# Half-filled contraction chunks in a conditioned attention and feed-forward block: zero padding to 128 rows, a new order of half and full matmuls, and a rebuilt passage between the two parts

## Chip, cores, metric

One core of one Trainium2 chip. The metric is the device time of one execution in microseconds (us). Times are quoted as the median and the range of the runs. A ratio is the mean time of one kernel's runs over that of the other's in the same rounds, so it is not quite the ratio of the medians that I quote. The span of a profiled execution is some 1.7 us shorter than the time of the same run (488.3 against 490.01 for the kernel before); spans are compared with spans and times with times.

Words used below: PE is TensorE's matmul, PEld its weight load, DVE VectorE, ACT ScalarE, POOL GpSimd. The "passage" is the time from the last key/value tile of attention to the first matmul of the feed-forward part (FFN). The "fold" multiplies the key and query weights by w_phi at the start, with "block weights" that GpSimd makes; a "num group" is the ten matmuls that give one tile's attention numerators; an "eviction" copies a matmul's result out of PSUM; a "half pair" is two matmuls of 64 rows side by side.

## The reference

```python
S, D, H, Dh, Dff = 2048, 576, 32, 18, 4608          # bf16 inputs, one batch
mod = silu(c) @ w_mod                                # six vectors sa, ca, ga, sb, cb, gb of 576
h = layernorm(x) * (1 + ca) + sa
q, k, v = split(h @ wqkv)                            # 32 heads of 18
phi(u) = concat(softmax(u @ w_phi), softmax(-u @ w_phi))
kv, z = phi(k)^T v, sum_s phi(k)                     # linear attention
o = (phi(q) kv) / (phi(q) z + 1e-6)
x = x + ga * (o @ wo)
h = layernorm(x) * (1 + cb) + sb
x = x + gb * (relu(h @ w1) @ w2)
```

What matters is that D = 576 = 4 x 128 + 64. Both kernels contract over at most 128 rows in one matmul, so each product over D has four full chunks and a half one of 64 rows.

## The kernel before

The half chunk is packed. Two 64-row matmuls, one on rows 0 to 63 and one on rows 64 to 127, go to two outputs and run side by side. The weights' last 64 rows therefore lie in SBUF twice.

```python
def paired(ps, lhs, rhs, splits, first=True):        # k, v, output projection
    for bk, (c0, cn) in enumerate(splits):
        for ci in range(4):
            nc.tensor.matmul(ps(bk)[:, 0:cn], lhsT=lhs(ci, 0, P), rhs=rhs[:, ci, c0:c0 + cn], ...)
    for bk, (c0, cn) in enumerate(splits):
        b0 = 64 * bk
        nc.tensor.matmul(ps(bk)[:, 0:cn], lhsT=lhs(4, b0, b0 + 64), rhs=rhs[b0:b0 + 64, 4, c0:c0 + cn], ...)

def mod_columns(parts, dst, psum):                   # one-column matmuls: 2 parts x 6 column groups x 5 chunks
    ...
                    for ck in range(NC):
                        k = KR[ck]                   # 128, 128, 128, 128, 64
                        nc.tensor.matmul(ps[p0:p0 + pn, n * NC + ci:n * NC + ci + 1],
                                         lhsT=wmod_sb[i][0:k, ck, ci * P:ci * P + pn], rhs=siluc[0:k, ck:ck + 1], ...)

def ffn(b, steps):                                   # b = 0..4; blocks of 256, 512, 512, 512, 256 tokens
    ...
    for j in range(NJ // 2):                         # 18 steps
        pace(9 * nn / 2400)                          # other tiles' work is inserted here by an estimate of time
        pair = (j, j + NJ // 2)
        for n, jj in enumerate(pair):                # eight full matmuls
            for ci in range(4):
                nc.tensor.matmul(hps[n][:, 0:nn], lhsT=w1a[:, ci, jj * P:(jj + 1) * P], rhs=h2T[:, ci, 0:nn], ...)
        for n in range(2):                           # then one half pair
            b0 = 64 * n
            nc.tensor.matmul(hps[n][:, 0:nn], lhsT=w1b[b0:b0 + 64, j * P:(j + 1) * P],
                             rhs=h2T[b0:b0 + 64, 4, 0:nn], start=False, stop=True)
        for n, jj in enumerate(pair):                # Relu: one on ScalarE, one on VectorE
            ...
```

While the FFN runs on block b, the attention output of block b+1 (`num_tile`, `tr_tile`, `wo_tile`) is inserted into TensorE's stream. Tiles 0 and 1 have no FFN to hide behind: they make up the passage.

The softmax here doesn't subtract the row's maximum and nothing guards it: scores larger than these inputs give would overflow.

Of the kernel before, what the change touches and what calls it, by code (L numbers as in the profile page):

```python
# [8 lines left out]
P = 128  # L9
# [9 lines left out]
NC = 5  # L19
# [16 lines left out]
def kernel(  # L36
# [74 lines left out]
    xn = small([P, NX, D], BF16, "xn")  # L111
# [7 lines left out]
    o_sb = small([P, NO, D], BF16, "o_sb")  # L119
# [11 lines left out]
    def load_rows(eng, dst, src, dup):  # L131
        eng.dma_start(dst[:, 0:4, :], src[0:512, :].rearrange("(k p) n -> p k n", p=P))
        eng.dma_start(dst[0:64, 4, :], src[512:576, :])
        if dup:
            eng.dma_start(dst[64:128, 4, :], src[512:576, :])
# [4 lines left out]
    for k in range(NC):  # L140
# [3 lines left out]
    load_rows(nc.sync, wmod_sb[0], w_mod[:, 0:D], False)  # L144
    load_rows(nc.sync, wmod_sb[1], w_mod[:, D:2 * D], False)
    load_rows(nc.sync, wv_sb, A_wqkv[:, 2 * D:3 * D], True)
    nc.sync.dma_start(x_sb[:, 4:8, :], xf[:, 4:8, :])
    load_rows(nc.sync, wq_raw, A_wqkv[:, 0:D], False)
    nc.sync.dma_start(x_sb[:, 8:16, :], xf[:, 8:16, :])
    load_rows(nc.sync, wmod_sb[2], w_mod[:, 2 * D:3 * D], False)  # L150
    load_rows(nc.sync, wo_sb, A_wo, True)
# [9 lines left out]
                            base=DH - 1, pattern=[[DH, 7]], channel_multiplier=-1)  # L161
    nc.gpsimd.memset(v_sb[:, :, 0:4, 126:127], 1.0)
# [25 lines left out]
    KR = [128, 128, 128, 128, 64]  # L188

    def mod_columns(parts, dst, psum):  # L190
        ps = psum()
        for n, i in enumerate(parts):
            for ci in range(NC):
                for p0, pn in ((0, P),) if ci < 4 else ((0, 64), (64, 64)):
                    for ck in range(NC):
                        k = KR[ck]
                        nc.tensor.matmul(ps[p0:p0 + pn, n * NC + ci:n * NC + ci + 1],  # L197
                                         lhsT=wmod_sb[i][0:k, ck, ci * P:ci * P + pn], rhs=siluc[0:k, ck:ck + 1],
                                         start=(ck == 0), stop=(ck == NC - 1))
        nc.vector.tensor_copy(out=dst[:, 0, :], in_=ps[:, 0:NC])  # L200
        nc.vector.tensor_scalar(out=dst[:, 1, :], in0=ps[:, NC:2 * NC], scalar1=1.0, scalar2=None, op0=ALU.add)

    def mod_row(i, dst, psum):
        for hf in range(2):
            ps = psum()
            for ck in range(NC):
                k = KR[ck]
                nc.tensor.matmul(ps[:, 0:HD2], lhsT=rep[0:k, ck, :],
                                 rhs=wmod_sb[i][0:k, ck, hf * HD2:(hf + 1) * HD2],
                                 start=(ck == 0), stop=(ck == NC - 1))  # L210
            nc.scalar.activation(out=dst[:, hf * HD2:(hf + 1) * HD2], in_=ps[:, 0:HD2], func=ACT.Copy)
# [9 lines left out]
    def fold_transposes(raw, dstT, engs):  # L221
        t0, t1 = two(), two()
        pts = [p.bitcast(BF16) for p in (t0[:, 0, :], t0[:, 1, :], t1[:, 0, :], t1[:, 1, :], one())]
        for ci in range(NC):
            for g, (h0, nh) in enumerate(GRP):
                f0, nf = h0 * DH, nh * DH
                if ci < 4:
                    nc.tensor.transpose(pts[g][0:nf, ci * P:(ci + 1) * P], raw[:, ci, f0:f0 + nf], ident[:, :])
                else:
                    for r in range(2):  # L230
                        nc.tensor.transpose(pts[g][0:nf, 512 + 64 * r:576 + 64 * r], raw[0:64, 4, f0:f0 + nf],
                                            ident[0:64, 0:64])
        for g, (h0, nh) in enumerate(GRP):
            nf = nh * DH
            if engs[g % len(engs)] == "a":
                nc.scalar.activation(out=dstT[0:nf, g, :], in_=pts[g][0:nf, 0:640], func=ACT.Copy)
            else:
                nc.vector.tensor_copy(out=dstT[0:nf, g, :], in_=pts[g][0:nf, 0:640])
# [27 lines left out]
    def ln_apply(n, t):  # L266
        return nc.vector.tensor_scalar(out=xn[:, t % NX, :], in0=x_sb[:, t, :],
                                scalar1=rs[:, n, t, 0:1], scalar2=rs[:, n, t, 1:2],
                                op0=ALU.mult, op1=ALU.add)
# [3 lines left out]
    def feat_t(t0, nt, psum, n):  # L273
        pt = psum().bitcast(BF16).rearrange("p (c f) -> p c f", c=2)
        for k, ci in enumerate(CS[n]):
            for j in range(nt):
                x = xn[:, (t0 + j) % NX, :]
                if ci < 4:
                    nc.tensor.transpose(pt[:, k, j * P:(j + 1) * P], x[:, ci * P:(ci + 1) * P], ident[:, :])  # L279
                else:  # L280
                    for r in range(2):
                        nc.tensor.transpose(pt[64 * r:64 * r + 64, k, j * P:(j + 1) * P], x[:, 512:576], ident[:, :])  # L282
# [16 lines left out]
    def paired(ps, lhs, rhs, splits, first=True):  # L299
        for bk, (c0, cn) in enumerate(splits):  # L300
            for ci in range(4):
                nc.tensor.matmul(ps(bk)[:, 0:cn], lhsT=lhs(ci, 0, P), rhs=rhs[:, ci, c0:c0 + cn],  # L302
                                 start=(first and ci == 0), stop=False)
        for bk, (c0, cn) in enumerate(splits):
            b0 = 64 * bk
            nc.tensor.matmul(ps(bk)[:, 0:cn], lhsT=lhs(4, b0, b0 + 64), rhs=rhs[b0:b0 + 64, 4, c0:c0 + cn],  # L306
                             start=False, stop=True)
# [4 lines left out]
    def k_tile(t):  # L312
        ps = two()
        paired(lambda bk: ps[:, bk, :], lambda ci, a, b: hT[a:b, ci, t * P:(t + 1) * P], wk_sb, HALF)
# [5 lines left out]
    def v_tile(t):  # L320
        ps = two()
        paired(lambda bk: ps[:, bk, :], lambda ci, a, b: hT[a:b, ci, t * P:(t + 1) * P], wv_sb, VSPL)
# [5 lines left out]
    def k_softmax(t):  # L328
# [8 lines left out]
        for sgn, eng in ((1, nc.gpsimd), (0, nc.vector)):  # L337
# [5 lines left out]
    def kv_tile(t):  # L343
        for g, (h0, nh) in enumerate(GRP):
            f0, nf = h0 * DH, nh * DH
            for sgn in range(2):
# [20 lines left out]
    def q_mm(b, n, psum):  # L367
        sl = slice(b * TB, (b + 1) * TB)
        pss = psum(len(QG[n]))
        for k, g in enumerate(QG[n]):  # L370
            f0, nf = GRP[g][0] * DH, GRP[g][1] * DH
            for ci in range(4):
                nc.tensor.matmul(pss[k][0:nf, :], lhsT=wq_sb[:, ci, f0:f0 + nf], rhs=hT[:, ci, sl],  # L373
                                 start=(ci == 0), stop=False)
        for k, g in enumerate(QG[n]):
            f0, nf = GRP[g][0] * DH, GRP[g][1] * DH
            b0 = 64 * k
            nc.tensor.matmul(pss[k][0:nf, :], lhsT=wq_sb[b0:b0 + 64, 4, f0:f0 + nf],  # L378
                             rhs=hT[b0:b0 + 64, 4, sl], start=False, stop=True)
# [39 lines left out]
    for n in range(3):  # L419
        feat_e(pts[n], 4, hT, 0, mod1, "vavav", n)  # L420
    order.close()
    nc.sync.dma_start(wmod_sb[3][:, 0:4, :], w_mod[0:512, 3 * D:4 * D].rearrange("(k p) n -> p k n", p=P))
    nc.sync.dma_start(wmod_sb[3][0:64, 4, :], w_mod[512:576, 3 * D:4 * D])
    load_rows(nc.sync, wmod_sb[5], w_mod[:, 5 * D:6 * D], False)

    QT = {4: (0, 0), 5: (0, 1), 7: (0, 2), 8: (1, 0), 9: (1, 1), 11: (1, 2), 12: (2, 0), 13: (2, 1), 15: (2, 2)}

    def a_filler(t):
        if t == 0:
            fold_transposes(wq_raw, wqT, "av")  # L430
            load_rows(nc.sync, wmod_sb[4], w_mod[:, 4 * D:5 * D], False)
# [12 lines left out]
    for t in range(NT + 1):  # L444
        if t < NT:
# [3 lines left out]
            if u < NT:  # L449
# [6 lines left out]
                if u % 4 == 3:  # L456
                    to_features(u - 3, 4, one, hT, (u - 3) * P, mod1, "avava", 0)
# [4 lines left out]
        if t < NT:  # L462
            if t + 4 < NT and t % 4 == 3:
                for n in (1, 2):
                    to_features(t + 1, 4, one, hT, (t + 1) * P, mod1, "avava", n)
# [4 lines left out]
    kv_tile(NT - 1)  # L470
    for k in range(2):
        q_exp(3, 0, q3[0], k)
    for g in range(NG):
        kv_final(g)
    actx.close()
# [13 lines left out]
    bctx = ExitStack()  # L489
    n3 = bctx.enter_context(tc.tile_pool(name="n3", bufs=2, space=PS, reuse_waits="tile"))  # L490
    s1 = bctx.enter_context(tc.tile_pool(name="s1", bufs=2, space=PS, reuse_waits="tile"))
# [16 lines left out]
    def num_mm(t, psum):  # L508
# [7 lines left out]
        for sgn in range(2):  # L516
            for g in range(3):
# [18 lines left out]
    def num_o(t, ps, adder):  # L536
# [22 lines left out]
        adder.tensor_tensor(out=o_sb[:, t % NO, :], in0=tm[:, 0, :], in1=tm[:, 1, :], op=ALU.add)  # L559
# [6 lines left out]
    def tr_tile(t, psum):  # L566
        pt = psum().bitcast(BF16)
        ot = o_sb[:, t % NO, :]
        for ci in range(4):
            nc.tensor.transpose(pt[:, ci * P:(ci + 1) * P], ot[:, ci * P:(ci + 1) * P], ident[:, :])  # L570
        for r in range(2):
            nc.tensor.transpose(pt[64 * r:64 * r + 64, 512:640], ot[:, 512:576], ident[:, :])  # L572
        nc.scalar.activation(out=oT[:, t % NO].rearrange("p c f -> p (c f)"), in_=pt[:, 0:640], func=ACT.Copy)  # L573

    def wo_mm(t, pss, first=True):
        f = oT[:, t % NO]
        paired(lambda bk: pss[bk], lambda ci, a, b: f[a:b, ci, :], wo_sb, HALF, first=first)
# [29 lines left out]
    def feat(b, n, psum):  # L607
        t0, nt = FB[b]
        to_features(t0, nt, psum, h2T, 0, mod2, "vavav", n)

    def ffn(b, steps):
# [11 lines left out]
        for j in range(NJ // 2):  # L623
            pace(9 * nn / 2400)
            pair = (j, j + NJ // 2)
            hps = [psf(), psf()]
            for n, jj in enumerate(pair):
                for ci in range(4):
                    nc.tensor.matmul(hps[n][:, 0:nn], lhsT=w1a[:, ci, jj * P:(jj + 1) * P], rhs=h2T[:, ci, 0:nn],  # L629
                                     start=(ci == 0), stop=False)  # L630
            for n in range(2):
                b0 = 64 * n
                nc.tensor.matmul(hps[n][:, 0:nn], lhsT=w1b[b0:b0 + 64, j * P:(j + 1) * P],  # L633
                                 rhs=h2T[b0:b0 + 64, 4, 0:nn], start=False, stop=True)
            for n, jj in enumerate(pair):
                if n == 0:
# [32 lines left out]
    def q_n3(n):  # L669
        ps = num3()  # L670
        return [ps[:, i, :] for i in range(n)]

    nps = [num_mm(0, num3)]
    num_d(0, nps[0])
    q3[1] = q_mm(3, 1, q_n3)
    num_o(0, nps[0], nc.vector)
    q_exp(3, 1, q3[1], 0)
    tr_tile(0, one_a)
    nps.append(num_mm(1, num3))
    num_d(1, nps[1])  # L680
    q_exp(3, 1, q3[1], 1)
    xps = [wo_x_mm(0, num3)]
    wo_mm(0, [xps[0][:, i, :] for i in range(2)], first=False)
    num_o(1, nps[1], nc.vector)
# [3 lines left out]
    mod_columns((3, 4), mod2, one_a)  # L688
    tr_tile(1, one_a)
    xps.append(wo_x_mm(1, num3))  # L690
    wo_mm(1, [xps[1][:, i, :] for i in range(2)], first=False)
    wo_x_stats(1, xps[1])
    ln_rstd(1, 1, 2)
    ln_apply(1, 1)
    mod_row(5, gb_row, one_a)
    q3[2] = q_mm(3, 2, lambda n: [one_a()])
# [65 lines left out]
```

## Time and profile before

| | kernel before |
|---|---|
| time, median of 15 runs | 488.58 us (487.25 to 490.8) |
| span of the profiled run, mean granted clock | 488.3 us, 0.965 |
| last key/value tile ends | 114.2 us |
| first FFN matmul | 140.2 us |
| first matmul of FFN block 1 (the first with 512 columns) | 195.8 us |

The profile's main lines are in the prediction. To read a row of stages: the stretch in us from the start, its length, then busy us of PE, PEld, DVE, ACT and POOL with the number of instructions, then the granted clock of TensorE (1.00 is full, 0.50 half), then DMA share and GB/s. These are the rows of the kernel before. The marks are the start of VectorE's key softmax (its sum, L331) for tile 0 and for tile 4, the end of the last key/value tile, the first FFN matmul, and the first of FFN block 1:

```profile
24.50:53.20 28.70, 23.34 (x205) 14.90 (x205) 24.93 (x57) 16.51 (x47) 5.12 (x4) 0.88 0.25 75
53.20:114.20 61.00, 59.67 (x476) 36.60 (x475) 38.21 (x48) 42.31 (x88) 18.42 (x12) 1.00 0.24 89
...
140.20:196.00 55.80, 53.17 (x443) 37.17 (x443) 30.10 (x87) 14.76 (x45) 5.61 (x4) 0.94 0.22 76
196.00:488.30 292.30, 288.06 (x2036) 175.31 (x2046) 124.25 (x289) 59.48 (x138) 14.05 (x10) 1.00 0.03 9
```

The first row, the passage (in the prediction) and the third have a clock below 1; the long row has PE busy for 288 of 292 us at full clock.

### The profile page before, as it was taken

The page shows a single profiled execution, that of the slowest core. Times are in us where ns is not written, and L with a number is a line of the kernel's source. Part 1 is how long each engine was busy: PE and PEld are TensorE (multiplying, and loading weights), DVE is VectorE, ACT ScalarE, POOL GpSimd, SP SyncE. Part 2 cuts the span into 40 slices and gives each one's busy share as a digit, 9 for nine tenths or more (in the row PEclk, how much of TensorE's full clock was granted, in tenths as well). Part 3 has the DMA queues.
Part 4 walks back from the last instruction along what each step waited for, and adds up shares of the span by engine and source line. Part 5 has one row for each costly group of instructions (what it writes and reads, how often), then busy time and mean ns, then how long its engine had stood idle before and what let it go on. Part 6 is the DMA issues. An engine that isn't in the chain of part 4 may idle for free.

```text
span 488.3 us, 8270 instructions
## 1 busy us (share of the span) xinstructions
PE 464.0 (95%) x3506; PEld 292.3 (60%) x3518; DVE 243.5 (50%) x565; ACT 154.2 (32%) x367; POOL 48.1 (10%) x59
## 2 busy tenths in 40 slices
PE   7978999997869999999999999999999999999997
PEld 6654566564536677334677733467773337777675
DVE  4597865656545654323655433365543332654312
ACT  4465686574333321223211122221112220112300
POOL 3012132231001110000211000021100000110000
PEclk9598999998888999999999999999999999999999
DMA  8950550000084000000000000000000000000000
GB/s 234 343 178 1 219 217 1 1 1 3 1 304 132 1 0 14 13 0 1 0 13 13 13 13 1 0 1 13 13 13 12 1 0 1 26 12 13 1 1 25
DMA packets 17312, 22.67 MB, mean 46 GB/s; under 512 B 2043, under 2 KB 16635, under 8 KB 16763
## 3 DMA queue, kind: packets, MB, share of 16 engines
q1 hardware_dynamic: 16064, 22.12, 13.6%
q8 instruction: 27, 0.44, 0.4%
q10 hardware_dynamic: 1210, 0.02, 0.2%
q14 instruction: 11, 0.08, 0.1%
HBM read 19.78 MB, written 2.36 MB: 45 GB/s over the span
## 4 chain that ended last, share of the span: by engine, by line
PE 72%; ACT 1%; DVE 1%; POOL 0%; issue 0%; POOLq 0%
PE psf L647 30%; PE psf L629 28%; PE psf L633 5%; PE psf L302 3%; PE num L514 2%; PE s L197 1%; PE pt L570 1%; PE psf L306 1%; PE psf L279 1%; PE n L302 1%; PE pt L572 1%; POOL o_sb L559 0%; PE psf L282 0%; DVE h2T L293 0%; ACT h2T L290 0%
## 5 line engine op out<-in xcount | busy, mean ns | idle before, releaser
L629 PE MATMUL psf<-h2T,rW 128*128 128x512 bf16 (+1 forms) x708 | 142.3, 341 | 1.1 <-DVE h2T L293 0.5
L647 PEld LDWEIGHTS <-rH 128*128 128x128 bf16 x1152 | 109.2, 98 | 29.6 <-issue 0.7
L647 PE MATMUL psf<-rW,rH 128*128 128x288 bf16 x864 | 116.8, 286 | 0.0
L639 DVE TENSOR_SCALAR rH<-psf 128x512 bf16<-128x512 f32 (+1 forms) x90 | 52.4, 583 | 97.4 <-PE psf L633 97.4
L629 PEld LDWEIGHTS <-rW 128*128 128x128 bf16 x720 | 64.4, 99 | 58.0 <-issue 11.9
L637 ACT ACTIVATE rH<-psf 128x512 bf16<-128x512 f32 (+1 forms) x90 | 46.1, 512 | 127.3 <-PE psf L633 127.3
L559 POOL TENSOR_TENSOR o_sb<-rV 128x576 bf16<-128x576 f32 x14 | 19.7, 1405 | 296.1 <-DVE rV L555 296.1
L302 PE MATMUL two<-rW,rH 128*128 128x288 bf16 (+2 forms) x256 | 42.8, 309 | 2.3 <-DVE rH L252 0.7
L650 DVE TENSOR_TENSOR yt<-psf,gb_row 128x288 f32<-128x288 f32 x32 | 14.5, 454 | 60.4 <-PE psf L647 60.4
L647 PE MATMUL psf<-rEQ,rH 128*128 128x288 bf16 x288 | 41.0, 286 | 0.0
L331 DVE TENSOR_REDUCE R_sb<-rH 128x64 f32<-128x1152 bf16 x16 | 21.6, 1351 | 23.8 <-ACT rH L317 23.7
L302 PEld LDWEIGHTS <-rH 128*128 128x128 bf16 x256 | 24.1, 104 | 14.0 <-issue 3.9
L339 POOL TENSOR_TENSOR rH<-rH,R_sb 128x576 bf16<-128x576 bf16 x16 | 23.5, 1474 | 81.2 <-ACT R_sb L334 41.5
L633 PE MATMUL psf<-h2T,rW 64*128 64x512 bf16 (+1 forms) x180 | 31.4, 346 | 0.0
L633 PEld LDWEIGHTS <-rW 64*128 64x128 bf16 x180 | 8.6, 93 | 30.9 <-issue 30.9
L261 ACT ACTIVATE rs<-mv,eps_t 128x1 f32<-128x1 f32 (+2 forms) x24 | 7.1, 294 | 62.7 <-DVE mv L258 60.2
L257 DVE BATCH_NORM_STATS2 st<-x_sb 128x6 f32<-128x288 bf16 x60 | 24.3, 439 | 3.3 <-DMA x_sb<-in_A_x_dram 3.3
L317 ACT ACTIVATE rH<-two 128x576 bf16<-128x576 f32 x32 | 19.3, 663 | 9.0 <-PE two L306 7.8
L386 ACT ACTIVATE rEQ<-two 126x512 bf16<-126x512 f32 (+1 forms) x34 | 17.7, 600 | 11.6 <-PE two L378 11.6
L573 ACT ACTIVATE oT<-pt 128x640 bf16<-128x640 bf16 x14 | 9.9, 704 | 35.6 <-PE pt L572 35.3
L339 DVE TENSOR_TENSOR rH<-rH,R_sb 128x576 bf16<-128x576 bf16 x16 | 17.5, 1096 | 0.7
L373 PE MATMUL two<-rH 128*126 128x512 bf16 (+1 forms) x68 | 16.5, 382 | 0.6 <-ACT rH L317 0.6
(135 smaller groups left out, 407.5 us busy)
## 6 DMA issues: line engine op xcount, KB each, us to landing
rW<-in_B_w_dram SPq DMA_DIRECT2D x1, 4608.0 KB
rW<-in_B_w_dram SPq DMA_DIRECT2D x3, 1296.0 KB, 9.0
rW<-in_w_mod_dram SPq DMA_DIRECT2D x6, 576.0 KB, 8.0
out_dram<-x_sb SPq DMA_DIRECT2D x16, 144.0 KB, 1.7
rEQ<-in_B_w_dram SPq DMA_DIRECT2D x1, 1296.0 KB
rW<-in_A_wqkv_dram SPq DMA_DIRECT2D x2, 576.0 KB, 9.7
x_sb<-in_A_x_dram SPq DMA_DIRECT2D x1, 1152.0 KB, 10.2
rW<-in_A_wqkv_dram SPq DMA_DIRECT2D x4, 144.0 KB, 3.0
```

What stands on the lines that cost most here:

```text
L257: nc.vector.bn_stats(out=s[:, hf, :], in_=x_sb[:, t, hf * HD2:(hf + 1) * HD2])
L302: nc.tensor.matmul(ps(bk)[:, 0:cn], lhsT=lhs(ci, 0, P), rhs=rhs[:, ci, c0:c0 + cn], start=(first and ci == 0), stop=False)
L317: nc.scalar.activation(out=E[:, sgn, :].rearrange("p (b f) -> p b f", b=2), in_=ps[:, :, 0:HD2], func=ACT.Exp, scale=1.0 - 2.0 * sgn)
L331: nc.vector.tensor_reduce(out=R[:, 0, :], in_=E, axis=AXX, op=ALU.add)
L339: eng.tensor_tensor(out=e, in0=e, in1=R[:, 1, sgn * H:(sgn + 1) * H].unsqueeze(2).to_broadcast([P, H, DH]), op=ALU.mult)
L386: nc.scalar.activation(out=Eq[b][0:nf, g, sgn, :], in_=pss[k][0:nf, :], func=ACT.Exp, scale=1.0 - 2.0 * sgn)
L559: adder.tensor_tensor(out=o_sb[:, t % NO, :], in0=tm[:, 0, :], in1=tm[:, 1, :], op=ALU.add)
L629: nc.tensor.matmul(hps[n][:, 0:nn], lhsT=w1a[:, ci, jj * P:(jj + 1) * P], rhs=h2T[:, ci, 0:nn], start=(ci == 0), stop=False)
L633: nc.tensor.matmul(hps[n][:, 0:nn], lhsT=w1b[b0:b0 + 64, j * P:(j + 1) * P], rhs=h2T[b0:b0 + 64, 4, 0:nn], start=False, stop=True)
L637: nc.scalar.activation(out=H1[:, jj, 0:nn], in_=hps[n][:, 0:nn], func=ACT.Relu)
L639: nc.vector.tensor_relu(H1[:, jj, 0:nn], hps[n][:, 0:nn])
L647: nc.tensor.matmul(ps[:, 0:cn], lhsT=H1[:, j, tt * P:(tt + 1) * P], rhs=w2q[j // 9][:, j % 9, c0:c0 + cn], start=(j == 0), stop=(j == NJ - 1))
```

## The change

Intent: TensorE pays each time its stream changes between 128-row and 64-row work (0.107 us in the prediction's trace). The change removes such switches by two means (1 and 2), rebuilds two stretches where TensorE waits (3 and 4), and moves work between engines (4 and 5).

1. Padding. Outside the FFN the last chunk becomes a full one, with zeros in rows 64 to 127, for k, v, q, the output projection, the feature transposes and the modulation vectors. GpSimd writes the zeros in 11 memsets at the start, and a twelfth later. For the FFN's own features there are no zeros: VectorE writes the last 64 columns twice, so that one full transpose gives both copies that the half pairs need.
2. FFN order. Steps alternate between full, half and half, full, so two half pairs stand together and a step has one switch instead of two.
3. Passage. The modulation set for the second norm, a query group and the order of tiles 0 and 1 are moved into waits; PSUM pools are swapped.
4. FFN block 0: both Relus on ScalarE, and inserted tiles spaced by the block's length.
5. In attention, VectorE takes over GpSimd's half of the softmax product.

Smaller moves come with it: other loop orders in `kv_tile` and `num_mm`, and another split of the feature evictions between ScalarE and VectorE.

```diff
-        for bk, (c0, cn) in enumerate(splits):
-            for ci in range(4): ...            # paired(): four full chunks, then a 64-row pair
+        for bk, (c0, cn) in enumerate(splits):
+            for ci in range(NC):               # project(): five full chunks
+                nc.tensor.matmul(ps(bk)[:, 0:cn], lhsT=lhs(ci), rhs=rhs[:, ci, c0:c0 + cn],
+                                 start=(first and ci == 0), stop=(ci == NC - 1))
 ...                                            # likewise q_mm, feat_t, tr_tile, row_mm
-                        k = KR[ck]
-                                         lhsT=wmod_sb[i][0:k, ck, ci * P:ci * P + pn], rhs=siluc[0:k, ck:ck + 1],
+                                         lhsT=wmod_sb[i][:, ck, ci * P:ci * P + pn], rhs=siluc[:, ck:ck + 1],
 ...
+    for z in zeros:                            # 11 slices
+        nc.gpsimd.memset(z, 0.0)
 ...
-        for sgn, eng in ((1, nc.gpsimd), (0, nc.vector)):
+        for sgn, eng in ((0, nc.vector), (1, nc.vector)):
 ...
+            for half in (0, 1) if j % 2 == 0 else (1, 0):      # ffn(): full,half | half,full | ...
+                last = half == (j + 1) % 2
+                for n, jj in enumerate(pair): ...
-                if n == 0:
+                if n == 0 or b == 0:
                     nc.scalar.activation(out=H1[:, jj, 0:nn], in_=hps[n][:, 0:nn], func=ACT.Relu)
 ...
-            gap = 7.5
-            us0 = total - 10 - gap * nt
+            gap = min(7.5, (total - 9) / nt)
+            us0 = total - 9 - gap * nt
 ...
     q3 = {0: q_mm(3, 0, q_two)}
     kv_tile(NT - 1)
+    mod2_ps = mod_mm((3, 4), one)              # was between tiles 0 and 1 of the passage
 ...                                            # passage: num 0, num 1, three query groups, then tiles 0 and 1
```

## The prediction

> **What bounds the kernel now.** I read the page first: the totals and the slices.
>
> ```profile
> PE 464.0 (95%) x3506; PEld 292.3 (60%) x3518; DVE 243.5 (50%) x565; ACT 154.2 (32%) x367; POOL 48.1 (10%) x59
> ...
> PE   7978999997869999999999999999999999999997
> ...
> PEclk9598999998888999999999999999999999999999
> ```
>
> TensorE is busy nearly everywhere, so what counts is its instruction stream, and where its clock or its inputs fail. The windows by stage show where:
>
> ```profile
> 26.00:56.00 30.00, 24.64 (x202) 15.15 (x200) 26.21 (x61) 17.51 (x50) 5.82 (x5) 0.89 0.25 73
> 56.00:114.20 58.20, 56.87 (x462) 35.11 (x459) 35.52 (x44) 40.21 (x81) 17.72 (x12) 1.00 0.22 84
> 114.20:140.20 26.00, 19.40 (x168) 12.20 (x166) 13.31 (x43) 10.46 (x28) 0.00 (x0) 0.87 0.15 49
> 140.20:150.70 10.50, 7.87 (x47) 4.80 (x47) 3.77 (x11) 2.28 (x8) 1.40 (x1) 0.67 0.72 260
> 150.70:490.00 339.30, 333.36 (x2434) 207.68 (x2442) 150.58 (x365) 71.96 (x175) 18.27 (x13) 1.00 0.04 12
> ```
>
> (columns: PE, PEld, DVE, ACT, POOL busy, granted clock, DMA). From 26 to 56 us VectorE is nearly full (26.2 of 30); from 56 to 114 TensorE is; 114 to 140 is the passage from attention to the feed-forward part (FFN), a chain of latencies; 140 to 151 is the FFN's bad start; after that TensorE has no wait at all: the waits of PE after 150 are an empty list. In that part time falls only if the stream gets shorter. So I looked at the stream itself, in the timeline of PE:
>
> ```profile
> 202.27 0.39 PE L629 MATMUL psf<-h2T,rW 128*128 128x512 bf16 x1
> 202.50 0.38 PE L629 MATMUL psf<-h2T,rW 128*128 128x512 bf16 x1
> ...
> 204.11 0.39 PE L633 MATMUL psf<-h2T,rW 64*128 64x512 bf16 x2
> 204.43 0.39 PE L629 MATMUL psf<-h2T,rW 128*128 128x512 bf16 x1
> ```
>
> Eight full matmuls and one pair of 64-row ones make a step of 204.43 - 202.27 = 2.16 us. Full ones follow each other every 0.215 us, and the pair runs side by side, so nine slots of 0.2155 = 1.94 us would do. The other 0.21 us are lost at the two changes between 128-row and 64-row work, 0.107 us each. The pair's weight loads show the same: 0.42 us and then 0.23 us of PEld idle put down to "issue", where loads are otherwise hidden. The same toll stands around the transposes and the output projection:
>
> ```profile
> 236.64 0.39 PE L570 MATMUL pt<-ident,o_sb 128*128 128x128 bf16 x4
> 236.96 0.25 PE L572 MATMUL pt<-ident,o_sb 128*64 128x128 bf16 x2
> 237.14 0.30 PE L647 MATMUL psf<-rW,rH 128*128 128x288 bf16 x1
> ...
> 239.19 1.14 PE L302 MATMUL psf<-wo_sb,oT 128*128 128x288 bf16 x8
> 240.26 0.30 PE L306 MATMUL psf<-wo_sb,oT 64*128 64x288 bf16 x2
> 240.49 0.30 PE L647 MATMUL psf<-rW,rH 128*128 128x288 bf16 x1
> ```
>
> 0.50 us for one tile's transposes, 1.30 us for its projection. Last, the waits of PE:
>
> ```profile
> PE pt L570 <- POOL o_sb L559: 2.6, 1, 2.6
> ...
> PE n L514 <- DVE kvzd L360: 1.8, 1, 1.8
> ...
> PE n L582 <- ACT rEQ L386: 1.5, 1, 1.5
> ```
>
> All three lie between 114 and 147 us. Few microseconds, but the clock falls after them (0.50 in 148 to 150).
>
> **What the Trainium skill says.** "TensorEngine Tiling (Array Packing)", Key Properties: "Changing tiling mode (not just tile) drains the TensorE". The trace agrees, at 0.107 us a change. "TensorE: Matmul & The Clock Gate", Back-to-back issue gap, gives N/2.4 + 2.5 ns[...], 216 ns at 512 columns and 122.5 at 288; the trace has 215 and 123. Its Part 1 says that the array falls to half clock after an idle window of some 3.4 us and needs a busy one to come back; the trace has clock 0.50 after the stall at 144. "SBUF — State Buffer", Who interferes with whom: a VectorE instruction with two SBUF inputs contends with a GpSimd one that reads SBUF. L339, on both engines at once, takes 749 ns at its shortest on VectorE and 1720 at its longest.
>
> **The change part by part.**
>
> (a) FFN up-projection. The order becomes full, half, half, full: one change per step instead of two. There are 18 steps in each of 5 blocks: 90 x 0.107 = 9.6 us. In block 0 the built order puts inserted work between two half pairs twice, four extra changes: +0.4. Net 9.2. It supposes that half pairs follow each other without a drain. The one sequence of that kind in the trace, 64-row transposes at 26.1 us, starts one every 0.06 us, the pitch of 128-row ones (8 in 0.45), so I believe it.
>
> (b) Padding to 128 rows, FFN part, 14 tiles. The projection becomes 10 x 0.1225 = 1.225 instead of 1.30: 14 x 0.075 = 1.1 us. The transposes become 5 x 0.056 = 0.28 instead of 0.50: 14 x 0.22 = 3.1. The last feature transposes of four blocks save about 0.2 each: 0.8. Sum 5.0.
>
> (c) Padding in attention. A k or v tile costs 1.32 us now (106.83 to 108.15) and 1.225 after; for the 24 tiles from t = 4 on that is 2.3 us. For t below 4 VectorE or the loads set the pace, and I count nothing. A query pair goes from 2.19 to 10 x 0.2155 = 2.155, six times: 0.2. A single goes from 1.30 to 1.08, twice: 0.4. The third single leaves the stage: 1.3. Three feature groups: 0.5. Sum 4.7 us, if TensorE stays the bound. Here VectorE takes over GpSimd's half of the softmax product: 0.76 us more per tile, less what the contention cost. From 28 to 62 us six L339 took 8.1 us; twelve of 0.757 make 9.1. After 62 us it goes from 9.4 to 15.1 in 52 us, where VectorE waits 18.5 us on ScalarE. It fits. Against it stand 11 memsets on GpSimd before the fold's block weights, which PE already awaits 1.1 us: +0.5. Net 4.2.
>
> (d) The passage. I laid the new order out with the old durations, from the end of the last kv tile (114.2) and with a cold clock after the 60 one-column matmuls, which now fill the wait for kv_final (3.6 us, to 117.8). Two num groups of 1.07 us end at 120.0. The query groups are paced by ScalarE's exponentials, four pairs of 1.1 us from 122.0; the third ends at 125.4 and frees the bank for tile 0's transpose. Copy (0.7), projection to 127.8, statistics, copy and rstd to 130.0, xn at 130.8. Tile 1 follows by 2.5 us: projection to 130.5, statistics 131.6, xn 133.3, transposes and eviction 134.4. The FFN then starts at 134.4 instead of 140.19: 5.8 us.
>
> (e) The FFN's start. From 140.19 to 150.74 PE did three steps of 1.19, one tile's transposes (0.5) and one num group (0.57): 4.6 us of warm work in 10.5. The new pacing puts the first transposes 6.6 us behind their num group instead of about two steps, and the chain to them (num, ScalarE, VectorE, GpSimd) takes some 5 us with the Relus off VectorE. So the stall goes, and one cold window stays, about 2 us: gain 3.9. ScalarE takes both Relus of block 0, 2 x 0.38 = 0.76 per step of 1.09, plus 1.8 per tile; that fits, with some jams, +0.5. Net 3.4.
>
> Sum: 9.2 + 5.0 + 4.2 + 5.8 + 3.4 = 27.6; 488.4 - 27.6 = 460.8, so 461.
>
> **The rivals.** First: half pairs that follow each other do drain, or the second pair's weights are not loaded behind the first. Then (a) gives nothing and the time is 470. For it: both pairs need the same row groups. Against it: the pitch of 0.06 us above, and that column-half transposes (L282, eight in 0.41 us) flow too. One in eight. Second: VectorE becomes the bound in attention. It has 26.2 of 30 us before t = 4 already; if its extra work lands on the path and TensorE cools once more there, (c) turns into a loss of 1 to 2 us and the time is 466. Third: the passage is paced by something that I placed wrongly, ScalarE's queue above all, and the FFN starts no earlier: 466. Fourth, on the good side: the cold stretch at 35 to 41 us vanishes as well, worth 2 to 3 us: 458. That the padding costs more than it saves (two full matmuls in place of one pair) the trace speaks against: 0.245 us against 0.22 to 0.35.
>
> **Range and chances.** (a) and (b) rest on repeated, steady durations and make half of the gain; the first rival would take 9 us. (c) to (e) are chains with a clock that can fall, each good to 2 us or so, together 3 to 4. I take 454 to 469. Two per cent is 478.7; for that (a) and the passage must both fail. Faster 0.97, same 0.03, slower under 0.01.
>
> **What would show it.** Right: the timeline of a full FFN block repeats every 4.1 us for two steps (2 x 1.94 + 2 x 0.107), with four half matmuls together; up-projection lines with less PEld idle "issue" (about half of 30.9 + 11.9); one tile's transposes at 0.28 us and a projection at 1.23; no PE wait on the GpSimd add in block 0; first FFN matmul near 130 us on the new clock (134.4 less 4.2). Wrong: a period of 4.3 us (first rival); VectorE without idle time and PE waits on L346 before 60 us (second); an FFN start after 134 us (third).

## The result

| | before | changed |
|---|---|---|
| time, median | 488.58 us (15 runs) | 454.01 us (10 runs, 453.43 to 457.23) |
| ratio, 95% interval | | 0.9303 (0.9282 to 0.9325) |
| profiled span, clock | 488.3 us, 0.965 | 452.1 us, 0.985 |
| last key/value tile ends | 114.2 | 104.5 |
| first FFN matmul | 140.2 | 124.4 |
| first matmul of FFN block 1 | 195.8 | 171.0 |

The gain is 34.6 us by the medians. I had predicted 27.6; 454.01 lies only just inside the range of 454 to 469, and that it does is luck: six of the ten runs are at 453.43 to 454.15, the other four at 454.79 to 457.23.

The totals and the clock of the changed kernel:

```profile
PE 430.5 (95%) x3448; PEld 294.9 (65%) x3460; DVE 245.7 (54%) x582; ACT 158.8 (35%) x387; POOL 32.0 (7%) x55
...
PEclk8699999998999999999999999999999999999999
```

PE is still busy for 95% of the span: the stream got shorter, not emptier. And by stage, cut at the same marks:

```profile
22.29:46.00 23.71, 20.32 (x203) 15.66 (x203) 22.91 (x54) 16.49 (x46) 0.00 (x0) 1.00 0.38 113
46.00:104.50 58.50, 55.42 (x453) 41.14 (x453) 44.53 (x67) 41.12 (x88) 0.00 (x0) 1.00 0.23 90
104.50:124.40 19.90, 15.93 (x168) 10.78 (x167) 14.54 (x47) 11.70 (x33) 1.40 (x1) 0.91 0.07 13
124.40:171.00 46.60, 46.59 (x434) 36.40 (x434) 25.93 (x73) 19.83 (x62) 5.61 (x4) 1.00 0.33 113
171.00:452.10 281.10, 276.15 (x2018) 177.05 (x2027) 124.53 (x299) 59.13 (x138) 14.08 (x10) 1.00 0.03 9
```

Row by row against before: from the key softmax of tile 0 to that of tile 4, 28.7 becomes 23.7; the rest of attention 61.0 becomes 58.5; the passage 26.0 becomes 19.9; FFN block 0 55.8 becomes 46.6, with PE busy for all of it; blocks 1 to 4 292.3 become 281.1.

The FFN's new rhythm, in the timeline of PE (start, duration, line, shapes):

```profile
173.37 3.63 PE L638 MATMUL psf<-h2T,rW 128*128 128x512 bf16 x16
176.93 0.61 PE L643 MATMUL psf<-h2T,rW 64*128 64x512 bf16 x4
177.47 3.63 PE L638 MATMUL psf<-h2T,rW 128*128 128x512 bf16 x16
```

Sixteen full matmuls, then four half ones together; the period of two steps is 177.47 - 173.37 = 4.10 us, where it was 2 x 2.16 = 4.32. Next, one tile's transposes:

```profile
142.72 0.44 PE L574 MATMUL pt<-ident,o_sb 128*128 128x128 bf16 x5
143.00 1.04 PE L638 MATMUL psf<-h2T,rW 128*128 128x256 bf16 x8
```

They take 143.00 - 142.72 = 0.28 us instead of 0.50. One tile's projection:

```profile
145.17 1.39 PE L313 MATMUL psf<-wo_sb,oT 128*128 128x288 bf16 x10
146.40 1.04 PE L638 MATMUL psf<-h2T,rW 128*128 128x256 bf16 x8
```

It takes 146.40 - 145.17 = 1.23 us instead of 1.30. The modulation set of 60 one-column matmuls in the passage, before:

```profile
125.73 3.73 PE L197 MATMUL s<-siluc,rW 128*128 128x1 bf16 x60
```

and in the changed kernel:

```profile
104.53 1.61 PE L197 MATMUL one<-siluc,rW 128*128 128x1 bf16 x60
...
106.64 1.31 PE L518 MATMUL n<-kvzd,rEQ 126*128 126x140 bf16 x20 [0.50 <-DVE kvzd L367]
107.79 6.44 PE L380 MATMUL s<-rH 128*126 128x512 bf16 x20
114.07 0.44 PE L574 MATMUL s<-ident,o_sb 128*128 128x128 bf16 x5
...
122.79 0.35 PE L518 MATMUL num<-kvzd,rEQ 126*128 126x140 bf16 x3 [0.94 <-ACT gb_row L224]
```

The set fell from 3.73 to 1.61 us; I had carried the old duration over. The bracket at the end of a line is the idle time before it and what ended it. Last, the longest waits of PE in the changed kernel (line, releaser, total us, times, longest):

```profile
PE two L257 <- POOL rV L229: 3.1, 1, 3.1
PE two L313 <- ACT rH L301: 1.7, 3, 1.1
...
PE two L313 <- ACT rEQ L388: 1.1, 5, 0.3
```

No wait on the GpSimd add is left in FFN block 0. Two kinds have grown: the memsets hold the block weights (L229) back, so the fold waits 3.1 us where it waited 1.1 (`PE two L246 <- POOL rV L216: 1.1, 1, 1.1` before); and the k and v matmuls wait 2.8 us for ScalarE (rH 1.7, rEQ 1.1), where they waited 0.6.

### The profile page after: what moved, and what is told of

Same layout as the page of the kernel before. It is cut to its first block, busy times and chain, and to the rows that moved or that the text cites.

```text
span 452.1 us, 8163 instructions
## 1 busy us (share of the span) xinstructions
PE 430.5 (95%) x3448; PEld 294.9 (65%) x3460; DVE 245.7 (54%) x582; ACT 158.8 (35%) x387; POOL 32.0 (7%) x55
## 4 chain that ended last, share of the span: by engine, by line
PE 83%; ACT 6%; DVE 6%; POOL 2%; issue 1%; ACTq 0%; DVEq 0%; POOLq 0%
PE psf L657 31%; PE psf L638 28%; PE psf L643 5%; PE psf L313 4%; PE two L313 4%; PE two L380 3%; DVE R_sb L338 2%; ACT rH L324 2%; ACT rEQ L388 2%; PE num L518 2%; DVE rH L346 1%; PE s L380 1%; POOL rW L164 1%; PE psf L293 1%; PE pt L574 1%
## 5 line engine op out<-in xcount | busy, mean ns | idle before, releaser
L638 PE MATMUL psf<-h2T,rW 128*128 128x512 bf16 (+1 forms) x708 | 132.3, 336 | 1.8 <-issue 0.9
L657 PEld LDWEIGHTS <-rH 128*128 128x128 bf16 x1152 | 111.2, 98 | 27.4
L638 PEld LDWEIGHTS <-rW 128*128 128x128 bf16 x720 | 66.6, 98 | 62.1 <-issue 15.3
L647 ACT ACTIVATE rH<-psf 128x256 bf16<-128x256 f32 (+1 forms) x108 | 51.8, 490 | 105.0 <-PE psf L643 84.8
L649 DVE TENSOR_SCALAR rH<-psf 128x512 bf16<-128x512 f32 (+1 forms) x72 | 45.0, 625 | 79.0 <-PE psf L643 39.7
L313 PE MATMUL two<-rW,rH 128*128 128x288 bf16 (+2 forms) x320 | 44.7, 287 | 4.7 <-ACT rH L301 1.7
L313 PEld LDWEIGHTS <-rH 128*128 128x128 bf16 x320 | 30.7, 98 | 14.8 <-issue 3.1
L643 PE MATMUL psf<-h2T,rW 64*128 64x512 bf16 (+1 forms) x180 | 23.8, 339 | 0.0
L346 DVE TENSOR_TENSOR rH<-rH,R_sb 128x576 bf16<-128x576 bf16 x32 | 22.9, 753 | 0.6
L546 DVE TENSOR_TENSOR ab<-dz 128x70 f32<-128x70 f32 x16 | 3.7, 232 | 34.8 <-ACT dz L537 34.8
L313 PE MATMUL psf<-wo_sb,oT 128*128 128x288 bf16 x140 | 19.4, 286 | 0.0
L380 PEld LDWEIGHTS <-rH 128*126 128x126 bf16 (+1 forms) x100 | 13.6, 139 | 9.0 <-issue 2.8
```

The costliest lines, as they stand in the source:

```text
L313: nc.tensor.matmul(ps(bk)[:, 0:cn], lhsT=lhs(ci), rhs=rhs[:, ci, c0:c0 + cn], start=(first and ci == 0), stop=(ci == NC - 1))
L346: eng.tensor_tensor(out=e, in0=e, in1=R[:, 1, sgn * H:(sgn + 1) * H].unsqueeze(2).to_broadcast([P, H, DH]), op=ALU.mult)
L380: nc.tensor.matmul(pss[k][0:nf, :], lhsT=wq_sb[:, ci, f0:f0 + nf], rhs=hT[:, ci, sl], start=(ci == 0), stop=(ci == NC - 1))
L647: nc.scalar.activation(out=H1[:, jj, 0:nn], in_=hps[n][:, 0:nn], func=ACT.Relu)
L649: nc.vector.tensor_relu(H1[:, jj, 0:nn], hps[n][:, 0:nn])
L657: nc.tensor.matmul(ps[:, 0:cn], lhsT=H1[:, j, tt * P:(tt + 1) * P], rhs=w2q[j // 9][:, j % 9, c0:c0 + cn], start=(j == 0), stop=(j == NJ - 1))
```

## The experiments

Twelve runs were made; all gave correct results. Ten kernels were timed, all in the fast state; the kernel before was profiled twice more, as single runs of unknown state. Unless said otherwise, an edit is on the changed kernel, and the difference is against its median of 454.01 us. These medians come from other rounds, and on other chips. By the ratios to the kernel before in the same rounds, which are the better measure, the three clear losses below (8.9, 4.0 and 4.9 us) are 8.3, 3.3 and 3.8.

### The FFN order

```diff
-            for half in (0, 1) if j % 2 == 0 else (1, 0):
-                last = half == (j + 1) % 2
+            for half in (0, 1):
+                last = half == 1
```

> The changed kernel with the up-projection again always full, full, half, half. Theory (each change between 128-row and 64-row work costs 0.107 us): one more change per step, 90 steps, less the two places where inserted work split the half pairs: 463 us, and a full block's step again 2.16 us. Rival (the two-step period of 4.10 us comes from the padding or from the evictions): 454, as the changed kernel.

Measured: 462.88 us (462.55 to 464.07), ratio to before 0.9473 (0.945 to 0.9496); 8.9 us slower. In the trace a step takes 180.03 - 177.87 = 2.16 us again:

```profile
177.87 1.90 PE L638 MATMUL psf<-h2T,rW 128*128 128x512 bf16 x8
179.70 0.39 PE L643 MATMUL psf<-h2T,rW 64*128 64x512 bf16 x2
180.03 1.90 PE L638 MATMUL psf<-h2T,rW 128*128 128x512 bf16 x8
```

The order is worth about what 90 switches of 0.107 us less 0.4 make (9.2).

The same order put alone into the kernel before:

> The kernel before with only the new order full, half, half, full in the up-projection. Theory: 90 steps x 0.107 us less, with two or three places where inserted work costs two changes back: 479 to 480. Rival (the gain needs the rest of the change): over 484.

Measured: 480.18 us (478.43 to 480.54), ratio 0.9829 (0.981 to 0.9848), 8.4 us by the medians. So this part adds up with the rest: its gain is the same with and without the other parts, within the noise. The rival that half pairs which follow each other drain is out.

### The padding of transposes and output projection, alone

Edit, on the kernel before: `o_sb` 640 columns wide, zeros in it and in `wo_sb`, five full transposes, and

```diff
-        paired(lambda bk: pss[bk], lambda ci, a, b: f[a:b, ci, :], wo_sb, HALF, first=first)
+        for bk, (c0, cn) in enumerate(HALF):
+            for ci in range(NC):
+                nc.tensor.matmul(pss[bk][:, 0:cn], lhsT=f[:, ci, :], rhs=wo_sb[:, ci, c0:c0 + cn],
+                                 start=(first and ci == 0), stop=(ci == NC - 1))
```

> The kernel before with only the attention output's transposes and projection padded to 128 rows. Theory: per tile 0.22 us for the transposes and 0.075 for the projection, 14 tiles in the feed-forward part and two in the passage: 4.1 to 4.7 us less, 484 us. Rival (the padding's extra matmul eats what the missing changes give): 488.

Measured: 482.87 us (482.16 to 483.72), ratio 0.9879 (0.9851 to 0.9906), that is 4.6 to 7.3 us of gain by the interval. The expected 4.1 to 4.7 lies at its lower edge. The direction holds, and the traces place the excess. FFN blocks 1 to 4 take 480.4 - 190.8 = 289.6 us where the kernel before takes 292.5: 2.9 less, as ten tiles of 0.295 make. But attention, which this edit does not touch, ends at 109.0 instead of 111.0 in the repeats of the kernel before (see below). So the excess of 1 to 2 us does not show in the steady part; the profile has it in the execution's luck.

### The modulation sets

```diff
+                        k = P if ck < 4 else 64
-                                         lhsT=wmod_sb[i][:, ck, ci * P:ci * P + pn], rhs=siluc[:, ck:ck + 1],
+                                         lhsT=wmod_sb[i][0:k, ck, ci * P:ci * P + pn], rhs=siluc[0:k, ck:ck + 1],
```

> The changed kernel with the modulation matmuls' last chunk again of 64 rows (24 changes of mode in each set of 60 one-column matmuls). Theory: the set of 60 takes 3.6 us again instead of 1.6, twice; the time grows by 3 to 5 us, 457 to 459, and the clock comes back later in the first 25 us. Rival (the set is quicker because of its new order over columns, or because weights load faster): 454, the set at 1.6 us.

Measured: 458.05 us (457.88 to 458.35), ratio 0.9371 (0.9351 to 0.939); 4.0 us slower. The set in the passage:

```profile
106.89 3.74 PE L198 MATMUL one<-siluc,rW 128*128 128x1 bf16 x60
```

It has its old length again, in its new place, so neither the place nor the new order over the columns is what shortened it: the padding of the 64-row chunk is. Each set has 12 such chunks, so 24 switches; (3.73 - 1.61) / 24 = 0.088 us each. The passage grew from 19.9 (104.53 to 124.41) to 21.55 us (106.89 to 128.44), and the set at the start from 1.95 to 4.36 us.

The other way round, 128 rows for the sets in the kernel before (`k = P`, and memsets of the four slices after the block weights):

> The kernel before with only the modulation matmuls on 128 rows (24 changes of mode less in each set of 60). Theory A (these changes explain the quicker start and, through the clock, the vanished cold stretch at 35 to 41 us): both sets fall from 3.7 and 4.35 us to 1.6 and 2, the stretch is gone, 480 to 482. Theory B (the stretch has other causes): 484 to 485, stretch still there.

Measured: 486.34 us (484.82 to 486.68), ratio 0.9934 (0.9912 to 0.9957): 3.2 us less by the mean. Both sets take 2.2 us there, 2.1 and 1.5 less than in the first profile (the repeats have 4.34 us for the second set, as its clock is at half there), but at the start PE then waits 2.1 us for VectorE's eviction of features before the first key tile at 18.86, so that this half of the saving is not passed on. Expectation B was the nearer one.

### The rebuilt pacing and the Relus of FFN block 0

```diff
-            gap = min(7.5, (total - 9) / nt)
-            us0 = total - 9 - gap * nt
+            gap = 7.5
+            us0 = total - 10 - gap * nt
```

> The changed kernel with the old pacing (gap 7.5, total - 10 - gap x nt). Theory: the first transposes stand two or three steps behind their num group again; PE waits about 3 us for the GpSimd add and the clock falls once: 457.5 to 459. Rival (with the Relus off VectorE the chain is short enough): under 1 us of wait, 454.5.

Measured: 458.86 us (457.64 to 459.68), ratio 0.938 (0.9353 to 0.9407); 4.9 us slower. The old wait is back in PE's list, and after it the clock is 0.50 at 132 to 134:

```profile
PE pt L574 <- POOL o_sb L563: 2.5, 1, 2.5
```

The pacing alone removes the stall and the half-clock window behind it.

```diff
-                if n == 0 or b == 0:
+                if n == 0:
```

> The changed kernel with the Relus of the first feed-forward block split over ScalarE and VectorE again. Theory: with the new pacing nothing waits for VectorE there, no difference: 454. Rival (VectorE's Relus hold up the chain of num groups): PE waits for the GpSimd add, 455 to 457.

Measured: 455.34 us (454.49 to 456.96), ratio 0.9314 (0.9285 to 0.9343). No difference that the runs resolve, and no wait for GpSimd: once the pacing is right, which engine does the Relus in block 0 makes no difference that the time shows (block 0 takes 47.3 us in its one profile, against 46.6).

### The softmax product

```diff
-        for sgn, eng in ((0, nc.vector), (1, nc.vector)):
+        for sgn, eng in ((1, nc.gpsimd), (0, nc.vector)):
```

> The changed kernel with the negative half of the key softmax product again on GpSimd. Theory A (taking it off GpSimd is why the cold stretch at 35 to 41 us went): the stretch comes back and the time is 457 to 461. Theory B (the stretch went because the start is quicker; on VectorE, which is full from 26 to 56 us, the product costs more than the contention did): no cold stretch, 451 to 454.

Measured: 455.37 us (454.4 to 456.44), ratio 0.9316 (0.9289 to 0.9342): the same as the changed kernel. The last key/value matmuls start at 104.59 instead of 104.22, and no half-clock stretch came back in the 30s. With GpSimd, PE waits 1.5 us for GpSimd's half of the product (three times) and 0.9 for VectorE's; with VectorE alone 0.2. Neither a gain nor a loss of that move can be seen in the time.

### The memsets ahead of the block weights

Edit: only 4 of the 11 memsets before the block weights, the other 7 and some more of GpSimd's constants after them (`for z in zeros[0:4]`, the rest issued after `build_bdw()`).

> The changed kernel with the fold's block weights made on GpSimd ahead of seven of the eleven zero memsets. Theory (the wait of 3.1 us for GpSimd at 7 to 10 us is on the path and lets the clock fall): fold 1.5 to 2.5 us earlier, time 450 to 452.5. Rival (the loads of the modulation weights set when the first modulation set can start): the wait moves there, 454.

Measured: 455.69 us (455.15 to 455.79), ratio 0.9318 (0.9295 to 0.9341). The fold starts at 8.21 instead of 10.10, and PE then waits for data:

```profile
PE one L201 <- DMA rW<-in_w_mod_dram: 1.4, 1, 1.4
PE one L246 <- DMA rW<-in_A_wqkv_dram: 1.3, 1, 1.3
```

Then with some 70 dummy matmuls as well, to hold the clock up in the start:

> The changed kernel with the block weights first on GpSimd and some 70 dummy transposes' worth of 128-column matmuls between fold and modulation, to keep the clock up while PE waits. Theory (the start loses time to the half clock from 8 to 19 us): clock near 1 there, first key tile 1 to 2 us earlier, 451 to 453. Rival (the loads set the start): first key tile no earlier, 454 to 455.

Measured: 456.35 us (454.79 to 456.57), ratio 0.9332 (0.9311 to 0.9353). The clock is 1.00 from 10 to 16, and PE waits 3.2 us for the query weights' transfer. So the 3.1 us wait for the memsets costs nothing that these two runs can see: the loads arrive later still.

### Is the half-clock stretch at 35 to 42 us the kernel's or the execution's?

The profile of the kernel before has the clock at 0.55 from 35 to 42. The three experiments built on that kernel had 1.00 there, although none of them touches the loop over the key tiles. So I profiled the kernel before twice more, unchanged.

> The kernel before, unchanged, profiled again. Theory (the half-clock stretch at 35 to 42 us in the first profile of the kernel before is luck of that execution, as three kernels with the same attention stage do not show it): in at least one of the two repeats PE's clock is 1.00 in 35 to 42 us, the last key tile starts near 109.5 to 110.5 instead of 114.2 and the span is 485 to 487 us. Rival (the stretch belongs to the kernel before, and the padding of the heads' matmuls undoes it): the clock is near 0.55 there in both repeats and the span is 488 us again.

> The same kernel once more, for a second draw. Theory: clock 1.00 in 35 to 42 us in at least one of the two, span 485 to 487 us. Rival: near 0.55 in both, span 488 us.

Measured: 487.8 and 488.92 us; spans 486.1 and 487.2. The clock from 35 to 42 was 1.00 and 0.89 (with 0.69 from 32 to 35). Both end the last key/value tile at 111.0, not 114.2. But their first FFN matmul comes at 139.24 and 139.28, hardly before the 140.19 of the first profile: the clock was at half later on instead. The stages of the first of the two:

```profile
24.30:50.00 25.70, 20.31 (x203) 13.83 (x202) 24.56 (x57) 16.36 (x47) 5.13 (x4) 1.00 0.29 86
50.00:111.00 61.00, 59.67 (x476) 36.60 (x475) 38.19 (x48) 42.31 (x88) 18.41 (x12) 1.00 0.24 89
111.00:139.20 28.20, 20.28 (x167) 12.90 (x165) 13.40 (x43) 10.46 (x28) 0.00 (x0) 0.76 0.15 45
```

The stretch belongs to the execution. One execution loses 3.2 us in attention and less in the passage, another the reverse. My expectation of the last key tile held in both (it starts at 110.4), that of the clock in the first; the second repeat, with 0.69 and 0.89, lies between theory and rival in its clock, and its span of 487.2 is just above the theory's 487. So "before minus changed" by stage, from one profile each, puts some 3 us into the wrong stage.

No version beat the changed kernel.

## Why the prediction was right, and why it fell short

The direction and the sum's repeated terms held. The gain was 34.6 instead of 27.6. Here is each term, with the first profile of the kernel before and with its first repeat as the base. Of the six profiles with the old order of the passage, four have it 27.4 to 28.3 us long, the repeat among them; the first profile has 26.0, and the one with the short modulation set 25.4.

| stage | predicted | first profile | repeat |
|---|---|---|---|
| attention (end of last key/value tile) | 4.2 | 114.2 - 104.5 = 9.7 | 111.0 - 104.5 = 6.5 |
| passage | 5.8 | 26.0 - 19.9 = 6.1 | 28.2 - 19.9 = 8.3 |
| FFN block 0: (e), and a block's share of (a) and (b) | about 6.3 | 55.6 - 46.6 = 9.0 | 54.4 - 46.6 = 7.8 |
| FFN blocks 1 to 4: the rest of (a) and (b) | about 11.3 | 292.5 - 281.1 = 11.4 | 292.5 - 281.1 = 11.4 |
| sum | 27.6 | 36.2 | 34.0 |

(Block 0 is counted from the first FFN matmul to the first with 512 columns: 140.19 to 195.82, 139.24 to 193.64, 124.41 to 171.01. Its 6.3 are 1.5 of (a), four tiles of 0.295 and 0.2 of features from (b), and the 3.4 of (e).)

**(a) and (b), right.** For blocks 1 to 4 the prediction's own counts make 72 x 0.107 = 7.7 for the order, 10 tiles x 0.295 = 2.95, and 0.6 for features: 11.3 against 11.4 measured. The period of 4.10 us and the 0.28 us of the transposes are what was named. Two runs confirm the order's size, +8.9 and -8.4; blocks 1 to 4 alone grow by 7.6 us in the one (288.7 against 281.1) and shrink by 7.5 in the other (285.0 against 292.5), where 7.7 was forecast. One named sign was only half right: PEld's idle "issue" at the up-projection went from 42.8 to 30.8 us, not to half. It fell by half at the 64-row loads (30.9 to 15.5) and rose at the full ones (11.9 to 15.3), at no cost in time.

**(c), right in mechanism, mis-sized, and in two places.** From tile 4 on I had put 4.7 us of shorter stream. PE's busy time there fell by 59.67 - 55.42 = 4.25, close to it. But the stage shortened by only 61.0 - 58.5 = 2.5, because PE's idle time rose from 1.3 to 3.1 us: it now waits 1.9 us for ScalarE there (L313 on rH and rEQ above all) and 1.0 for VectorE. The clause "if TensorE stays the bound" was where this failed. The second place is the sentence "For t below 4 VectorE or the loads set the pace, and I count nothing". VectorE is nearly full there, as that says (24.56 of 25.7 us in the repeat, 22.91 of 23.7 after), and yet the stretch became shorter. Six of the seven profiles with the product on VectorE alone have it at 23.7 us; of the six with the old attention, four have it at 25.0 to 25.8, and the two with the lower clock there at 27.2 and 28.7. So it gave 1.3 to 2.0 us. With the product back on GpSimd it takes 24.4, so the softmax move may be some 0.7 of it; the rest was not separated. Before this stretch no gain is shown, though the key softmax of tile 0 begins 2.0 us earlier than in the repeat (24.30 to 22.29): it begins at 22.79 to 24.50 in the five profiles with the old start, and at 22.12 to 23.59 in the five with the new. The changed kernel's own profile is an early one. Three others with its attention end the last key/value tile at 105.7 to 105.8, so that attention's 6.5 against the repeat is rather 5.3. The modulation set at the start, which fell from 4.35 to 1.95 us, was not in my sum; with its 64-row chunks back, tile 0's key softmax begins at 24.66, later than in any of the five. The 2.0 us that the memsets add ahead of it are hidden, as their own runs show. The 0.5 for the memsets was too small as a wait (2.0 more) and too large as a cost (none seen).

**(d), the new passage right, by two errors that cancel; the old one mis-read.** I laid out 20.2 us and 19.9 were measured. Within it, the one-column set was 1.6 instead of 3.6 us, and everything behind it ran about 2 us early: tile 0's transposes at 9.5 after the start instead of 11.2, tile 1's projection ended at 14.5 (117.78 + 1.23 - 104.5) instead of 16.3. Then the tail took 5.4 instead of 3.9, with PE waiting for xn, x_sb, gb_row and h2T in turn, 0.4 to 0.9 us each. So the plan's first step failed: "with a cold clock after the 60 one-column matmuls, which now fill the wait for kv_final (3.6 us, to 117.8)" carries over a duration that the change itself cuts, since 24 of the removed switches lie there. Undoing that alone cost 4.0 us over both sets, and none of it was in my sum as a saving. The other error cancelled it. What made the 5.8 fall short is the other side of the difference: I took the old passage as 26.0, from one profile, and the repeats show 28.2 and 28.3.

**(e), right in mechanism, mis-sized.** I gave 3.9 for the stall less 0.5 for jams on ScalarE, and kept one half-clock window of 2 us. The changed kernel enters the FFN at full clock and never leaves it (1.00 in the row of block 0), and no jams show. Undoing only the pacing cost 4.9.

**The rivals.** Draining half pairs: refuted by two runs. VectorE as the bound: one half of its named sign came (VectorE is busy for 22.91 of the 23.71 us before tile 4), the other did not (no PE wait on L346 before 60 us); PE waits for ScalarE's evictions more than for VectorE, TensorE does not cool there, and (c) did not become a loss. A late FFN start: it came at 124.4, not after 134. The named 130 (134.4 less 4.2) was missed by 5.8 us, nearly all of it because attention ended at 104.5 and not at 110.0. The fourth, that the stretch at 35 to 41 us vanishes, looks confirmed when two profiles are laid side by side, and is not: it was gone from one repeat of the old kernel and weaker in the other (0.69 at 32 to 35, 0.89 at 35 to 42), at spans only 1 to 2 us shorter. So the sentence that valued it at 2 to 3 us mistook an execution's luck for a property of the kernel.

**Two readings that prove less than they were made to.** The 64-row transposes at 26.1 us, taken as a sign that half pairs do not drain, are 64 columns wide, and the ones that they are compared with 128: an equal pitch says little. The two runs on the order decide it. And the stall at 144, set beside the idle window of some 3.4 us in the Trainium skill ("TensorE: Matmul & The Clock Gate", Part 1), kept PE idle for only 2.63 us before the clock fell; in the changed kernel the clock is 0.50 at 108 to 110 although PE had no wait over 0.50 us from 104 on. What lets the clock fall these traces do not settle.

**What stays open.** The excess over the sum is 34.6 - 27.6 = 7.0. Against the repeat, attention holds 2.3 of it, the passage 2.5, block 0 1.5: 6.3, and 0.6 is left between spans and medians. Some 1.2 of attention's part is the early start of the changed kernel's profile; how much of the rest is the clock's luck, I cannot tell from single profiles. No run undoes the new order of the passage by itself, or the padding of k, v and q alone: their shares are read from profiles, not shown by an experiment.

## What to carry to other kernels

When a change removes a cost per switch, count the switches everywhere, small instructions first: here 24 of them made more than half of a set of 60 tiny matmuls, and its old duration was carried into the new plan. Take the size of a chain of latencies from more than one profile of the old kernel, because a half-clock window can lie in it in one execution and elsewhere in the next. And once the busiest engine's stream gets shorter, expect to give part of the gain back in waits for the others: here 4.25 us less work gave 2.5.

## What the Trainium skill lacked or had wrong

- "TensorEngine Tiling (Array Packing)", Key Properties, says that a change of tiling mode drains TensorE and gives no size. The runs show 0.107 us a change in a stream of 512-column matmuls, and 0.088 us in the one-column sets ((3.73 - 1.61) / 24).
- The same page, Theoretical Speedup, gives "Up to 2×" for a dimension of up to 64. It doesn't say that a lone pair between full matmuls can save nothing: eight full and one pair took 2.16 us at 512 columns, as much as ten full ones (10 x 0.2155 = 2.155), and at 288 columns 1.30 against 1.225. Only two pairs in a row paid (2.05 us a step).
- "TensorE: Matmul & The Clock Gate", Back-to-back issue gap, gives about 131 ns per 512-column matmul for a sustained stream with weight loads, and 216 for an isolated one. The stream here, with a weight load for each matmul, shows 215 ns: the figure that the section calls isolated holds in the stream.
- The same page, Part 1, tells of run-to-run variation at the start of a kernel. Here it was in the middle too: three profiles of one kernel had half clock at 35 to 42 us, or from some 117 to 131, the last key/value tile ended at 114.2 or 111.0, and the spans were 486.1 to 488.3.
